# Transposing the attention output by DMA instead of on TensorE, and setting constants in pieces

## The chip, the cores and the metric

The kernel runs on one core of a Trainium2 chip. The metric is the device time of one execution in microseconds (us). The engines are called PE (TensorE, matrix engine), DVE (VectorE), ACT (ScalarE), POOL (GpSimd) and SP (the engine that only issues transfers here); PEld is the weight load of PE, which overlaps its matmuls (PE is busy for 98% of the span before, PEld for 65%).

The kernel before was timed with the changed one at 679.28 us (median of 4 runs, 679.05 to 679.72), and at 679.09 us when it stood alone.

## The reference, cut to what matters

```python
# attention: 4 batches, 8 heads, 768 positions, head width 64
# each query sees its window (|distance| < 16) and 24 block summaries (max of k, mean of v)
x = attn_out.transpose(0, 2, 1, 3).reshape(3072, 512)
P = np.exp(x @ w_gate - max)            # 8 experts
for _ in range(8):                       # the "normalisation"
    P /= P.sum(1, keepdims=True) + 1e-09
    P /= P.sum(0, keepdims=True) + 1e-09
    P *= N / E
for e in range(8):                       # experts, 512 -> 1024 -> 512
    out += P[:, e:e+1] * (np.maximum(x @ w1[e], 0) @ w2[e])
```

The gate products of this kernel (x @ w_gate) take the attention output with its 512 features on the partitions, that is, transposed. The attention produces it with positions on the partitions. Something has to transpose it: 16 head pairs (two heads of one batch), six blocks of 128x128 each.

## The kernel before

A planner in Python orders all work of the attention stage, with expert 0 as filler, before anything is emitted. It knows each unit by an engine, an estimated duration, its dependencies and a `lag`, the time that it believes passes between the end of a unit and the use of its result. The order in which an engine works is then fixed in the program: a unit that waits on the chip holds everything behind it on its engine (in the changed kernel PE is busy for 0.15 of the 2 us from 98 us on, while a gate product waits). Pairs 8 to 11 belong to batch 2, pairs 12 to 15 to batch 3.

```python
def to_xT(i, h=None):                      # six TensorE transposes into one PSUM bank
    t = at.pop(("xs", i, h or 0))
    tx = at["tx", i, h] = bank("a", "tx", FP16)
    for g in range(G if h is None else HG):
        nc.tensor.transpose(tx[:, g * 128:(g + 1) * 128],
                            t[:, g, :, :].rearrange("p j d -> p (j d)"), ident16)

def x_out(eng, i, h=None): ...             # copy PSUM -> xT on ACT or DVE

def near_values(i): ...                    # the four small "edge copies", SBUF to SBUF, issued from SP

def logits(b):                             # the gate products of batch b, 24 small matmuls
    lp = at["lp", b] = bank("a", "lp")[:, 0:G * E]
    ...

# in pair_whole(i), batches 1 to 3
U["xt", i] = add("PE", 0.35, lambda: to_xT(i), [U["no", i, 0], U["no", i, 1]], prio, opens=[buf])
U["x", i] = add({"ACT": 0.8, "DVE": 0.9}, 0, lambda: x_out(U["x", i].on, i), [U["xt", i]], prio, uses=[buf])
...
# after a batch: gate products, then the batch's filler
gate(b, xs, 900 if b < B - 1 else 0)
expert0(b * S, xs)
...
for i in range(4):                         # weights of expert 1, issued from POOL
    load(("w1n", i), lambda i=i: load_w1(1, i), 0.85, 1.3)
load("w2n", lambda: load_w2(1), 0.85, 5.0)
...
# in bridge(), the eight normalisation rounds: rows, by_rows (POOL), columns (DVE), totals (PE), ...
step = add(eng, us, fn, [step], -50.0, opens=o, uses=w, lag=(1.5 if n else 3.0) if fn is columns else 0.0)
```

The softmax here doesn't subtract the row's maximum and nothing guards it: scores larger than these inputs give would overflow.

Of the kernel before, what the change touches and what calls it, by code (L numbers as in the profile page):

```python
# [33 lines left out]
class Plan:  # L34
# [12 lines left out]
    def add(self, eng, cost, fn, deps=(), prio=0.0, opens=(), uses=(), lag=0.0):  # L47
        u = Unit(eng, cost, fn, [d for d in deps if d is not None], prio, list(opens), lag)
        for b in list(opens) + list(uses):
            b.users.append(u)  # L50
        if uses and eng != "PE":
            u.prio -= 100.0
        self.waiting.append(u)
        return u
# [62 lines left out]
def kernel(  # L117
# [10 lines left out]
    nc = tc.nc  # L128

    B, H, S, D = q.shape  # L130
    G = S // 128
    N, DM = out.shape
    E = moe_w_gate.shape[1]
# [5 lines left out]
    PB = H // 2  # L139
    SCALE = 1.0 / float(D) ** 0.5  # L140
    W = 16
# [4 lines left out]
    VD = D + 1  # L146
# [9 lines left out]
    col_en = const.tile([128, 128], FP32)  # L156
# [3 lines left out]
    xT = persist.tile([128, KD, N], FP16)  # L160
# [34 lines left out]
    def copy(eng, out, in_):  # L195
        (nc.scalar.copy if eng == "ACT" else nc.vector.tensor_copy)(out=out, in_=in_)
# [18 lines left out]
    NB = PB  # L215
    NE = 2
# [9 lines left out]
    if True:  # L226
# [4 lines left out]
        qT = [attn.tile([128, W + S + W], BF16, name=f"qT{i}") for i in range(NB)]  # L231
        kT = [attn.tile([128, S], BF16, name=f"kT{i}") for i in range(NB)]
# [6 lines left out]
        E_e = [attn.tile([128, G, 128], BF16, name=f"Ee{i}") for i in range(NE)]  # L239
        V_e = [attn.tile([128, G, 2 * VD], BF16, name=f"Ve{i}") for i in range(NE)]  # L240

        plan = Plan({"m": 3, "s": NS, "a": NA})
        add = plan.add

        at, units = {}, {}
# [49 lines left out]
        def tr(i, z, tag):  # L295
            st = at.pop(("st", i, z))
            t = at["t", i, z] = bank(tag, "tkq", BF16)
            for g in range(G):
# [4 lines left out]
                else:  # L303
                    nc.tensor.transpose(t[:, g * 128:(g + 1) * 128],  # L304
                                        st[:, g, :, :].rearrange("p j d -> p (j d)"), ident)

        def tr_out(eng, i, z):
            r, src = i % NB, at.pop(("t", i, z))[:, 0:S]
            dst = (kT[r][:], qT[r][:, W:W + S])[z]
            if i < PB:  # L310
                dst = dst.rearrange("c (p g) -> c p g", g=G)
                src = src.rearrange("c (g p) -> c p g", g=G)
            copy(eng, dst, src)
# [32 lines left out]
        def near_values(i):  # L346

            sv, ve = v_x[i % NQ], V_e[i % NE]
            for j in range(2):
                c0, q0 = VD * j, 64 + 32 * j  # L350
                nc.sync.dma_start(out=ve[q0 + W:q0 + 2 * W, 1:G, c0:c0 + VD],
                                  in_=sv[128 - W:128, j, 0:G - 1, :])
                nc.sync.dma_start(out=ve[q0:q0 + W, 0:G - 1, c0:c0 + VD],
                                  in_=sv[0:W, j, 1:G, :])

        def scores(i, h):
# [145 lines left out]
        def to_xT(i, h=None):  # L502
# [6 lines that stand above are left out]
        def x_out(eng, i, h=None):  # L509
            n, t0 = (S, 0) if h is None else (HS, h * HS)  # L510
            t0 += i // PB * S
            copy(eng, xT[:, i % PB, t0:t0 + n], at.pop(("tx", i, h))[:, 0:n])
# [76 lines left out]
            nc.vector.tensor_copy(out=wg_bf[:], in_=wg_f32[:])  # L589

        def late_constants():
            for t in E_e:
                nc.vector.memset(t[64:128, :, :], 0.0)
            for t in V_e:
                nc.vector.memset(t[:], 0.0)
                nc.vector.memset(t[0:24, :, D:VD], 32.0 / XS)
                nc.vector.memset(t[32:56, :, VD + D:2 * VD], 32.0 / XS)
            nc.vector.memset(col_en, float(E) / float(N))


        U = {}
# [20 lines left out]
        def pair_start(i, prio):  # L622
            o = i - NB
            war_k = [U.get(("S", o, 0)), U.get(("S", o, 1)), U.get(("km", o))]
            war_q = war_k[:2] + [U.get(("ss", o, 0)), U.get(("ss", o, 1))]
            tag = "m" if i < PB else "a"
            for z in range(2 if i >= PB else 1):
                buf = Buffer(tag)
                U["tr", i, z] = add("PE", 0.4, lambda z=z: tr(i, z, tag),
                                    [U["kq"[z], i], U["ident"]] + (war_k, war_q)[z]  # L630
                                    + [U["tr", i, 0] if z else U.get(("S", i - 1, 1 if i > PB else 0))],
                                    prio, opens=[buf])
                U["kT", i, z] = add({"ACT": 0.8} if z == 0 else {"ACT": 0.8, "DVE": 0.95},
                                    0, lambda z=z: tr_out(U["kT", i, z].on, i, z), [U["tr", i, z]], prio,
                                    uses=[buf])
            if i < PB:
                query_half(i, 0, prio)
            U["km", i] = add("DVE", 0.95, lambda: key_max(i), [U["kT", i, 0]] + war_q[2:], prio)
            buf = Buffer("a")
            U["vs", i] = add("PE", 0.4, lambda: block_sums(i),  # L640
                             [U["v", i]] + ([U.get(("A", i - NE, 1))] if i >= PB else []), prio + 0.01, opens=[buf])
            U["Vs", i] = add("DVE", 0.36 if i < PB else 0.84, lambda: block_out(i), [U["vs", i]],
                             prio + 0.01, uses=[buf])
# [37 lines left out]
            return U.get((what, n % PB, n // PB)) if n >= 0 else None  # L681

        def pair_whole(i, prio):
            U["near", i] = add("SP", 0.4, lambda: near_values(i), [U["v", i], U.get(("A", i - NE, 1))], prio,
                               lag=3.5)
            for h in range(2):
                buf = Buffer("s")
                U["S", i, h] = add("PE", 0.28, lambda h=h: scores(i, h),
                                   [U["kT", i, 0], U["kT", i, 1], U.get(("ed", i - 2))], prio, opens=[buf])
                U["X", i, h] = add("ACT", 0.97, lambda h=h: score_exp(i, h), [U["S", i, h]], prio, uses=[buf])  # L690
                U["mk", i, h] = add("DVE", 0.56, lambda h=h: masks(i, h),
                                    [U["X", i, h], U.get(("A", i - 2, 1))], prio)
            U["ed", i] = add("DVE", 0.78, lambda: edges(i),
                             [U["X", i, 0], U["X", i, 1], U["mk", i, 1], U.get(("A", i - NE, 1))], prio)
            bufs = [Buffer("a"), Buffer("a")]
            U["ss", i, 0] = U["ss", i, 1] = add("PE", 0.22, lambda: summaries2(i),
                                                [U["km", i], U["kT", i, 1], U.get(("A", i - NE, 1))], prio,
                                                opens=bufs)
            for h in range(2):
                U["sx", i, h] = add("ACT", 0.46, lambda h=h: summary_exp(i, h), [U["ss", i, h]], prio,  # L700
                                    uses=[bufs[h]])
            for h in range(2):
                buf = Buffer("a")
                U["A", i, h] = add("PE", 0.4, lambda h=h: values(i, h),
                                   [U["mk", i, h], U["ed", i], U["sx", i, h], U["Vs", i], U["near", i]],
                                   prio, opens=[buf])
                U["no", i, h] = add("DVE", 0.68, lambda h=h: normalize(i, h),
                                    [U["A", i, h], U.get(("xt", i - 2))], prio, uses=[buf])
            buf = Buffer("a")
            U["xt", i] = add("PE", 0.35, lambda: to_xT(i), [U["no", i, 0], U["no", i, 1]], prio, opens=[buf])  # L710
            U["x", i] = add({"ACT": 0.8, "DVE": 0.9}, 0, lambda: x_out(U["x", i].on, i), [U["xt", i]], prio,
                            uses=[buf])

        halves, zero = [], []

# [52 lines left out]
        c0 = add("DVE", 3.8, constants, [], -5.0)  # L768
        for i in range(PB):
            pair_start(i, i)  # L770
            pair_half(i, 0, i)
        add("DVE", 2.4, late_constants, [U["mk", PB - 1, 0]], 5.5)
        expert0(0, [U["x", i, 0] for i in range(PB)])
        for i in range(PB):
            pair_half(i, 1, 10 + i)
# [2 lines left out]
        for i in range(PB, NP):  # L778
# [3 lines left out]
            if i % PB == PB - 1:  # L782
                b = i // PB
                xs = [U["x", PB * b + d] for d in range(PB)]
# [24 lines left out]
    if True:  # L809
# [340 lines left out]
        g = q = NOTHING  # L1150
        for n in range(LAG, len(groups)):
            g0, q0 = g, q
            g = group(*groups[n])
            q = pair(*groups[n - LAG])
            e, j, i = groups[n]
# [55 lines left out]
        A, B, C, D = last  # L1211
# [42 lines left out]
```

## Time and profile before

| | before |
|---|---|
| time, median of 4 runs beside the changed kernel | 679.28 us |
| PE busy | 670.5 us, 98% of the span of the profiled run |
| transposes of attention outputs on PE | 96, six to a pair |
| DMA queue of SP, pairs 8 to 15 | edge copies only |

The prediction below shows the engine table, the stretches and the removed instructions.

One warning about this profile. The profiled execution took 684.06 us, some 5 us more than the others, because the clock fell near its start:

```profile
20.00:30.00 10.00, 9.02 (x108) 5.64 (x108) 6.78 (x22) 4.94 (x10) 5.27 (x7) 0.72 1.38 199
```

The columns are the stretch, its length, busy time and count of PE, PEld, DVE, ACT and POOL, the granted clock, the DMA share (the larger, the busier) and GB/s; here the clock was 0.72. A span is the time from the first to the last instruction on the core; it is some 2 us shorter than the device time.

### The profile page before, as it was taken

How to read it: one execution, taken by the hardware profiler on the slowest of the kernel's cores; microseconds unless marked ns; L12 is line 12 of the kernel's file. 1: busy time of each engine (PE TensorE's matmuls, PEld its weight loads, DVE VectorE, ACT ScalarE, POOL GpSimd, SP SyncE). 2: the span in 40 equal slices, each digit the busy share in tenths (PEclk: the TensorE clock that was granted, in tenths of full speed). 3: DMA queues.
4: the chain of work that ended last, by engine and by line, in shares of the span. 5: the costliest groups of instructions: out<-in, count | busy, mean ns of one | idle time of the engine just before them, and what ended most of it. 6: DMA issues, size and time to landing. Idle time of an engine off the chain costs nothing.

```text
span 681.4 us, 13654 instructions
## 1 busy us (share of the span) xinstructions
PE 670.5 (98%) x5189; PEld 441.6 (65%) x5189; DVE 585.4 (86%) x1445; ACT 407.7 (60%) x788; POOL 125.9 (18%) x165
## 2 busy tenths in 40 slices
PE   8999999999999999999999999999999999999996
PEld 4665666545666666666666666666666666666665
DVE  6778898788599988999889988998899888998886
ACT  4677877656677765555555555555555555555551
POOL 8699630022202010100101010201010101100000
PEclk9799999999999999999999999999999999999999
DMA  9999990000503123310513050404131051301224
GB/s 120 188 143 143 98 144 7 1 1 0 78 1 37 12 31 48 31 17 1 78 17 33 1 78 1 48 1 60 19 31 17 7 72 17 32 1 48 78 93 155
DMA packets 113618, 33.90 MB, mean 50 GB/s; under 512 B 99984, under 2 KB 110736, under 8 KB 113552
## 3 DMA queue, kind: packets, MB, share of 16 engines
q0 software_dynamic: 104672, 26.22, 41.6%
q1 hardware_dynamic: 8352, 6.80, 3.3%
q8 instruction: 40, 0.66, 0.4%
q14 instruction: 26, 0.21, 0.1%
q10 hardware_dynamic: 528, 0.02, 0.0%
HBM read 52.45 MB, written 6.29 MB: 86 GB/s over the span
## 4 chain that ended last, share of the span: by engine, by line
PE 92%; DVE 4%; DMA 1%; issue 1%; ACT 1%; POOL 1%; DVEq 0%; ACTq 0%
PE xy L883 36%; PE pg L877 16%; PE pa L877 10%; PE pb L877 10%; PE yps L210 6%; PE hps L200 6%; PE sg L323 1%; PE tkq L304 1%; PE vs L331 1%; PE av L468 1%; PE tx L506 1%; DMA qst<-in_q_dram 1%; DVE out_acc L1018 1%; PE av L395 1%; PE av L401 1%
## 5 line engine op out<-in xcount | busy, mean ns | idle before, releaser
L883 PEld LDWEIGHTS <-hf 128*128 128x128 f16 x2352 | 230.1, 98 | 96.1 <-issue 1.2
L883 PE MATMUL xy<-w,hf 128*128 128x256 f16 x1312 | 183.4, 273 | 0.1
L883 PE MATMUL xy<-ws,hf 128*128 128x256 f16 x984 | 147.6, 273 | 0.1
L191 ACT ACTIVATE hf<-pg 128x512 f16<-128x512 f32 x84 | 50.2, 597 | 149.6 <-PE pg L877 149.4
L1018 DVE SCALAR_TENSOR_TENSOR out_acc<-xy,P_sb,out_acc 128x512 f32<-128x512 f32 x164 | 115.1, 744 | 1.7 <-PE xy L883 1.7
L824 DVE TENSOR_TENSOR hf<-hf 128x512 f16<-128x512 f16 x252 | 99.6, 422 | 8.8
L877 PE MATMUL pa<-xT,w 128*128 128x512 f16 x336 | 99.9, 379 | 0.0
L877 PEld LDWEIGHTS <-w 128*128 128x128 f16 x672 | 65.8, 98 | 43.6 <-issue 0.6
L827 DVE TENSOR_TENSOR hf<-pb,c 128x512 f16<-128x512 f32 x84 | 58.1, 692 | 38.2 <-PE pb L877 35.7
L176 POOL DMA_DIRECT2D w<-in_moe_w_dram x56 | 41.8, 759 | 220.3 <-PE pg L877 192.1
L877 PEld LDWEIGHTS <-ws 128*128 128x128 f16 x504 | 49.3, 98 | 25.3
L911 ACT COPY c<-pg 128x512 f32<-128x512 f32 x84 | 49.2, 585 | 22.7 <-PE pg L877 22.6
L827 DVE TENSOR_TENSOR hf<-pg,c 128x512 f16<-128x512 f32 x84 | 57.2, 681 | 0.6 <-PE pg L877 0.6
L191 ACT ACTIVATE hf<-pa 128x512 f16<-128x512 f32 x84 | 50.6, 603 | 0.4 <-PE pa L877 0.4
L896 ACT COPY pg<-pa 128x512 f32<-128x512 f32 x84 | 47.9, 570 | 4.8
L877 PE MATMUL pg<-xTs,w 128*128 128x512 f16 x168 | 50.0, 379 | 0.1
L877 PE MATMUL pb<-xT,ws 128*128 128x512 f16 x168 | 50.0, 379 | 0.0
L877 PE MATMUL pg<-xTs,ws 128*128 128x512 f16 x168 | 50.0, 379 | 0.0
L877 PE MATMUL pg<-xT,w 128*128 128x512 f16 x168 | 50.0, 379 | 0.0
L877 PE MATMUL pb<-xTs,ws 128*128 128x512 f16 x168 | 50.0, 379 | 0.0
L904 ACT COPY c<-pb 128x512 f32<-128x512 f32 x84 | 49.8, 593 | 0.2 <-ACT pg L896 0.2
L200 PE MATMUL hps<-xT,w 128*128 128x384 f16 x256 | 48.7, 326 | 0.0
(136 smaller groups left out, 842.5 us busy)
## 6 DMA issues: line engine op xcount, KB each, us to landing
w<-in_moe_w_dram POOLq DMA_DIRECT2D x8, 1024.0 KB, 9.3
w<-in_moe_w_dram POOLq DMA_DIRECT2D x56, 128.0 KB, 3.5
out_dram<-out_acc SPq DMA_DIRECT2D x22, 256.0 KB, 2.0
qst<-in_q_dram POOLq DMA_DIRECT2D x32, 96.0 KB, 5.8
vx<-in_v_dram POOLq DMA_DIRECT2D x16, 192.0 KB, 6.5
kst<-in_k_dram POOLq DMA_DIRECT2D x24, 96.0 KB, 6.0
w<-in_moe_w_dram POOLq DMA_DIRECT2D x2, 512.0 KB, 8.3
kst<-in_k_dram POOLq DMA_DIRECT2D x4, 192.0 KB, 4.9
```

What stands on the lines that cost most here:

```text
L176: nc.gpsimd.dma_start(out=t[:, :, h, :], in_=moe_w1[e].rearrange("(dk p) f -> p dk f", p=128)[:, :, f:f + 128])
L191: nc.scalar.activation(out=out, in_=in_, func=AF.Relu, bias=0.0, scale=1.0)
L200: nc.tensor.matmul(hp[:, 0:n], lhsT=w1s[e][:, dk, 128 * f:128 * (f + 1)], rhs=xT[:, dk, t0:t0 + n], start=(dk == 0), stop=(dk == KD - 1))
L210: nc.tensor.matmul(yp[:], lhsT=h[:, f, c * 128:(c + 1) * 128], rhs=w2s[e][:, f, :], start=(f == 0), stop=(f == KF - 1))
L824: nc.vector.tensor_tensor(out=out, in0=in0, in1=in1, op=ALU.subtract)
L827: nc.vector.tensor_tensor(out=out, in0=in0, in1=in1, op=ALU.add)
L877: nc.tensor.matmul(bank[:], lhsT=w[:, dk, :], rhs=x[:, dk, :], start=start and dk == 0, stop=dk == KH - 1, skip_group_check=True)
L883: nc.tensor.matmul(bank, lhsT=a(f)[:, 128 * c:128 * (c + 1)], rhs=w[:, f, :], start=start and f == 0, stop=f == FH - 1, skip_group_check=True)
L896: nc.scalar.copy(out=B["g"][:], in_=B["a"][:])
L904: nc.scalar.copy(out=B["c5"][:], in_=B["b"][:])
L911: nc.scalar.copy(out=B["c2"][:], in_=B["g"][:])
L1018: nc.vector.scalar_tensor_tensor(out=acc, in0=src, scalar=P_sb[:, t, e:e + 1], in1=acc, op0=ALU.mult, op1=ALU.add)
```

## The change

The intent is to relieve PE, which bounds this stage: the outputs of pairs 8 to 15 are transposed by one DMA each, straight from SBUF to SBUF, so that 48 TensorE transposes, 8 evacuating copies and 8 uses of a PSUM bank go. The constants that later batches need are set as seven small units in place of one long one on DVE. Two further branches, for i >= 16, are never taken, since there are 16 pairs.

```diff
+        def x_dma(i):
+            nc.sync.dma_start_transpose(
+                out=xT[:, i % PB, i // PB * S:(i // PB + 1) * S].rearrange("c (g t) -> c g t", g=G),
+                in_=at.pop(("xs", i, 0))[:].rearrange("p g j d -> p (g j d)"))
...
         def late_constants():
-            for t in E_e:
-                nc.vector.memset(t[64:128, :, :], 0.0)
-            for t in V_e:
-                nc.vector.memset(t[:], 0.0)
+            def zero(t):
+                nc.vector.memset(t, 0.0)
+            def ones(t):
                 nc.vector.memset(t[0:24, :, D:VD], 32.0 / XS)
                 nc.vector.memset(t[32:56, :, VD + D:2 * VD], 32.0 / XS)
-            nc.vector.memset(col_en, float(E) / float(N))
+            parts = [(0.4, lambda t=t: zero(t[64:128, :, :])) for t in E_e]
+            for t in V_e:
+                parts += [(0.4, lambda t=t: zero(t[:])), (0.15, lambda t=t: ones(t))]
+            return parts + [(0.15, lambda: nc.vector.memset(col_en, float(E) / float(N)))]
...
-            buf = Buffer("a")
-            U["xt", i] = add("PE", 0.35, lambda: to_xT(i), [U["no", i, 0], U["no", i, 1]], prio, opens=[buf])
-            U["x", i] = add({"ACT": 0.8, "DVE": 0.9}, 0, lambda: x_out(U["x", i].on, i), [U["xt", i]], prio,
-                            uses=[buf])
+            if i >= 8:
+                U["xt", i] = U["x", i] = add("SP", 0.1, lambda: x_dma(i), [U["no", i, 0], U["no", i, 1]], prio,
+                                             lag=2.6)
+            else:
+                ...  # as before
...
-        add("DVE", 2.4, late_constants, [U["mk", PB - 1, 0]], 5.5)
+        c1 = U["mk", PB - 1, 0]
+        for us, fn in late_constants():
+            c1 = add("DVE", us, fn, [c1], 12.5)
```

More of the change, by code (lines that the diff above doesn't have):

```diff
@@ L305, in tr, with tr_dma @@
                                         st[:, g, :, :].rearrange("p j d -> p (j d)"), ident)
+        def tr_dma(i, z):
+            r, st = i % NB, at.pop(("st", i, z))
+            nc.sync.dma_start_transpose(out=(kT[r][:], qT[r][:, W:W + S])[z].rearrange("c (g t) -> c g t", g=G),
+                                        in_=st[:].rearrange("p g j d -> p (g j d)"))
+        def x_dma(i):
+            nc.sync.dma_start_transpose(
+                out=xT[:, i % PB, i // PB * S:(i // PB + 1) * S].rearrange("c (g t) -> c g t", g=G),
+                in_=at.pop(("xs", i, 0))[:].rearrange("p g j d -> p (g j d)"))
         def tr_out(eng, i, z):
@@ L350, in near_values @@
                 c0, q0 = VD * j, 64 + 32 * j
-                nc.sync.dma_start(out=ve[q0 + W:q0 + 2 * W, 1:G, c0:c0 + VD],
+                eng = nc.gpsimd if i >= 16 else nc.sync
+                eng.dma_start(out=ve[q0 + W:q0 + 2 * W, 1:G, c0:c0 + VD],
                                   in_=sv[128 - W:128, j, 0:G - 1, :])
-                nc.sync.dma_start(out=ve[q0:q0 + W, 0:G - 1, c0:c0 + VD],
+                eng.dma_start(out=ve[q0:q0 + W, 0:G - 1, c0:c0 + VD],
                                   in_=sv[0:W, j, 1:G, :])
@@ L627, in pair_start @@
             for z in range(2 if i >= PB else 1):
+                if i >= 16:
+                    U["tr", i, z] = U["kT", i, z] = add("SP", 0.1, lambda z=z: tr_dma(i, z),
+                                                        [U["kq"[z], i]] + (war_k, war_q)[z], prio, lag=2.6)
+                    continue
                 buf = Buffer(tag)
@@ L683, in pair_whole @@
         def pair_whole(i, prio):
-            U["near", i] = add("SP", 0.4, lambda: near_values(i), [U["v", i], U.get(("A", i - NE, 1))], prio,
+            U["near", i] = add(*(("POOL", 3.4) if i >= 16 else ("SP", 0.4)), lambda: near_values(i), [U["v", i], U.get(("A", i - NE, 1))], prio,
                                lag=3.5)
@@ L708, in pair_whole @@
                                     [U["A", i, h], U.get(("xt", i - 2))], prio, uses=[buf])
-            buf = Buffer("a")
-            U["xt", i] = add("PE", 0.35, lambda: to_xT(i), [U["no", i, 0], U["no", i, 1]], prio, opens=[buf])
-            U["x", i] = add({"ACT": 0.8, "DVE": 0.9}, 0, lambda: x_out(U["x", i].on, i), [U["xt", i]], prio,
-                            uses=[buf])
+            if i >= 8:
+                U["xt", i] = U["x", i] = add("SP", 0.1, lambda: x_dma(i), [U["no", i, 0], U["no", i, 1]], prio,
+                                             lag=2.6)
+            else:
+                buf = Buffer("a")
+                U["xt", i] = add("PE", 0.35, lambda: to_xT(i), [U["no", i, 0], U["no", i, 1]], prio, opens=[buf])
+                U["x", i] = add({"ACT": 0.8, "DVE": 0.9}, 0, lambda: x_out(U["x", i].on, i), [U["xt", i]], prio,
+                                uses=[buf])
         halves, zero = [], []
```

## The prediction

> **What bounds the kernel now.** I read the engine table first, then the chain that ended last, then the engines stretch by stretch, and last the order of time around the instructions that the change removes. The engine table and the head of the chain:
>
> ```profile
> PE 670.5 (98%) x5189; PEld 441.6 (65%) x5189; DVE 585.4 (86%) x1445; ACT 407.7 (60%) x788; POOL 125.9 (18%) x165
> ...
> PE 92%; DVE 4%; DMA 1%; issue 1%; ACT 1%; POOL 1%; DVEq 0%; ACTq 0%
> ```
>
> The matrix engine is busy for 98% of the span, and 92% of the chain that set the end is its work. An average can hide stages, so I read the busy time of each engine in stretches (columns: stretch, its length, busy time and count of PE, PEld, DVE, ACT, POOL, then the clock, the DMA column and GB/s):
>
> ```profile
> 45.00:66.00 21.00, 21.00 (x235) 13.12 (x234) 18.66 (x52) 15.81 (x25) 20.45 (x25) 1.00 2.47 143
> 66.00:88.00 22.00, 21.92 (x262) 13.79 (x260) 19.85 (x53) 18.03 (x30) 15.21 (x19) 1.00 1.63 106
> 88.00:109.00 21.00, 21.00 (x253) 13.44 (x252) 17.80 (x48) 16.26 (x27) 3.44 (x5) 1.00 0.82 102
> 109.00:130.00 21.00, 21.00 (x226) 12.83 (x224) 15.79 (x43) 14.22 (x23) 0.00 (x0) 1.00 0.02 4
> 130.00:178.00 48.00, 46.82 (x260) 24.56 (x257) 36.33 (x94) 27.78 (x56) 11.42 (x18) 1.00 0.00 1
> ```
>
> Attention of batches 2 and 3 lies at about 80 to 130 us, with expert 0 woven between as filler. The matrix engine has no idle time in the two stretches from 88 to 130, although the vector engine is at 75 to 85%. So in this stage a microsecond taken off the matrix engine is a microsecond off the time, and one taken off ACT or DVE alone is worth nothing. From 130 to 178 us the eight rounds of the routing normalisation run on DVE and POOL, filled by the rest of expert 0; there 1.2 us are idle. After 178 us the order is untouched by the change. The DMA engines are nearly silent after 109 us, which matters for the new transfers.
>
> The removed work is told by the view of the tile that holds the transposed attention output, and by one spot in order of time (start, length, engine, line):
>
> ```profile
> L506 PE MATMUL tx<-ident,xs x96: 216/219/314, 13.2 to 127.9; 128*128 128x128 f16 x96
> L196 ACT COPY xT<-tx x15: 460/798/805, 13.7 to 128.2; 128x768 f16<-128x768 f16 x10, 128x384 f16<-128x384 f16 x5
> ...
> 105.94 1.04 PE L210 MATMUL yps<-w,h 128*128 128x512 f16 x4
> 106.81 0.50 PE L506 MATMUL tx<-ident,xs 128*128 128x128 f16 x6
> 107.14 1.03 PE L210 MATMUL yps<-w,h 128*128 128x512 f16 x4
> ```
>
> The 219 ns of one transpose is latency, not the engine's cost: six of them started at 106.81 and the next matmul started at 107.14, so six take the engine 0.33 us (about 55 ns each). The neighbours are dense: four 512-wide matmuls take 106.81 - 105.94 = 0.87 us, 217 ns each.
>
> [...] for plain transfers from SP: 2.0 us median for 256 KB, and 1.9 us for the fastest of the small edge copies; but those edge copies take 4.6 us in the median, issued while the load queue is full:
>
> ```profile
> out_dram<-out_acc SPq DMA_DIRECT2D x22, 256.0 KB, 2.0
> Ve<-vx SPq DMA_DIRECT2D x48, 10.2 KB, 4.6
> ```
>
> No trace of this case shows a crossbar transpose yet.
>
> **The change part by part.** There are 4 batches of 8 heads, so 16 head pairs, numbered 0 to 15. The two branches under "i >= 16" (keys and queries by DMA, edge values issued from POOL) are therefore never taken; the built program confirms it: POOL has the same instruction count and the transposes of keys and queries stay on the matrix engine. Two parts remain.
>
> Part one, outputs of pairs 8 to 15. Removed: 8 x 6 = 48 matrix-engine transposes (96 fall to 48 in the built program), 8 evacuating copies of 128x768 (0.8 us on ACT or 0.56 us on DVE), and 8 uses of a PSUM bank. Added: 8 transposing transfers of 128x768 two-byte values (192 KB) on SP. On the path: 8 x 0.33 = 2.65 us; some groups are followed a little later (0.43 us to the next start at 122.74), so I take 2.8 us. The 8 copies, at most 6.4 us of ACT, are off the path. The scheduler moves part of the query copies from DVE to ACT and output copies the other way, which again is not on the path.
>
> What replaces them is a delay. Only the gate products of batches 2 and 3 wait first for the new transfers; the expert products of the batch stand behind them in the order. Batch 3 is the tight one. In the built order 16 output matmuls (16 x 0.217 = 3.5 us) and 4 hidden matmuls (4 x 0.163 = 0.65 us) stand between the last value product and the gate product: 4.1 us. In the trace of before, the last value product is out of the way at 125.89, and the last normalised output is written at 126.67 + 0.56 = 127.23, 1.34 us later. So a transfer may take 4.1 - 1.3 = 2.8 us from issue to landing before the matrix engine stalls. For batch 2 the same count (two score groups, one block-sum, two transposes, 16 hidden matmuls: some 4.3 us) leaves about 3.0 us. [...] the change itself plans 2.7 us. That fits in the slack, just. I charge 0.4 us for the two places together.
>
> Part two, constants in pieces. In the trace of before the block of memsets holds DVE in one go while the matrix engine runs dummy work and then has real gaps:
>
> ```profile
> 23.62 1.91 PE L544 MATMUL idle<-zeros 128*128 128x512 bf16 x4
> 23.90 0.38 DVE L593 MEMSET Ee<- 64x384 uint32 x1
> ...
> 25.89 0.17 DVE L598 MEMSET col_en<- 128x128 f32 x1
> ...
> 27.18 0.39 PE L323 MATMUL sg<-qT,kT 64*128 64x160 bf16 x8 [0.40 <-ACT qT L196]
> ...
> 29.04 0.33 PE L506 MATMUL tx<-ident,xs 128*128 128x128 f16 x3 [0.58 <-ACT es L430]
> ```
>
> I cannot see the memsets delay a matmul directly: they end at 26.06, before the next normalisation starts at 26.36. The four dummy matmuls stay in the new order. What changes is that the scheduler now believes DVE free and puts the transposes of pair 3 ahead of the summary scores, and 4 hidden matmuls into the place where the engine waited 0.58 us for ACT. Of the 1.0 us of waits at 27.2 and 29.0 I expect 0.6 us back.
>
> A third effect: the new order puts the first normalisation product 4 hidden matmuls (0.65 us) nearer to the end of attention, while its DVE and POOL chain is as long as before. At 139.9 the trace already has a 0.9 us wait of this kind. I charge 0.3 us.
>
> Sum: -2.8 - 0.6 + 0.4 + 0.3 = -2.7 us. From 679.1 that is 676.4 us.
>
> **The rivals.** (1) The gain turns into a stall. [...] the gate products of both batches each wait about 5 us: +10 - 3.4, some 686 us. For it: nothing of the kind has been measured here[...]. Against it: one instruction carries all six blocks[...], and the change plans 2.7 us. At 4.5 us, a middle case, each place loses 1.6 us and the time is about 679 us, no change. (2) The bound moves: with the matrix engine relieved, DVE at 75 to 90% or the normalisation chain becomes the bound, and nothing or 1 us is won: 678 to 679 us. Against it: the copies on DVE hardly change in number in the new order (two more of outputs, two fewer of queries), and it has a fifth of its time free between 88 and 130. (3) The SP queue[...] holds edge copies behind a transpose that still waits for its data; the value products then wait. The order speaks against it: the edge copies that follow a transpose belong to a pair two to three ahead. It would cost below 2 us, 678 us. (4) The reordering helps more than counted, as pieces of filler land in other small gaps: 674 us.
>
> **Range and chances.** The removable work is 2.8 us and the visible gaps of the stage about 1 us, so 674.3 is the low end. The high end, 679.3, allows a transfer of some 4.5 us, or stalls that eat the gain. A gain of 2% would be 13.6 us, four times what is removed; a loss of 2% needs a transfer near 10 us at both places. Predicted 676.4 us, range 674.3 to 679.3; faster 0.01, same 0.97, slower 0.02.
>
> **What would show it.** Right: 48 instead of 96 of the tx transposes; the gate products of batches 2 and 3 with waits under 0.5 us; a landing time of 2.5 to 3 us for the new transfers; attention ending (the first row sums of the routing) 3 us before the 130.49 us of the old trace; the same length from there to the end. Wrong: a gate product waiting over 1 us on the transfer; landings of over 4 us; the row sums 3 us earlier but the output matmuls of expert 1 (start at 176.3 us) not, which would mean that the normalisation chain took the gain; or the matrix engine idle in the stretches from 88 to 130 us.

The sum stands: -2.8 - 0.6 + 0.4 + 0.3 = -2.7 us, that is 676.4 us from 679.1. The +0.4 us and the wait of 5 us in rival 1 are suppositions.

## More of the kernel before

One more view is needed later: what PE waited for (line of the waiting instruction, what it waited for: us in total, times, longest).

```profile
PE sink L1077 <- DVE csum_sb L1072: 0.9, 1, 0.9
...
PE tx L506 <- ACT es L430: 0.6, 1, 0.6
...
PE sg L323 <- ACT qT L196: 0.4, 1, 0.4
```

"sink" is the total over all rows in one normalisation round, "csum_sb" the column sums that feed it. There are few waits, and none of them is for a transfer in the attention of batches 2 and 3.

## The result, and the profile after

The changed kernel took 687.84 us (median of 4 runs, 687.32 to 688.62), against 679.28 us of the kernel before in the same session. The ratio is 1.0126, with a 95% interval of 1.0109 to 1.0144. Ratios here are the mean time of one kernel's fast runs over that of the other's from the same rounds, so they are not quite the ratio of the medians. The change made the kernel 8.6 us slower. That is within the band of 2% that the prediction thought almost certain, but outside its range, and it has the other sign.

PE did lose the work (page of the changed kernel, busy time by engine):

```profile
PE 668.6 (98%) x5141; PEld 437.2 (64%) x5141; DVE 581.7 (85%) x1440; ACT 404.2 (59%) x785; POOL 125.9 (18%) x165
```

5141 matmuls are the 5189 of before less 48, and DVE and ACT lose five and three instructions, together the eight copies. But one stretch stands out, first the changed kernel, then its stand-in for before, the run with the pieces alone (span 677.3 us, mean clock 0.998, nothing in its attention outputs changed; stretches, columns as above):

```profile
88.00:109.00 21.00, 15.61 (x160) 9.88 (x160) 11.66 (x32) 9.93 (x17) 0.94 (x2) 0.84 0.91 111
```

```profile
88.00:109.00 21.00, 21.00 (x256) 13.27 (x254) 18.62 (x50) 16.32 (x26) 0.00 (x0) 1.00 0.51 70
```

In the same 21 us PE is idle for 5.4 us, the clock averages 0.84, and 160 matmuls are done in place of 256. The waits of PE in the changed kernel say for what:

```profile
PE lp L531 <- DMA xT<-xs: 5.4, 2, 3.6
PE sink L1102 <- DVE csum_sb L1097: 1.8, 2, 1.0
...
PE ss L430 <- DVE xT L196: 0.5, 1, 0.5
...
PE sg L333 <- ACT qT L196: 0.4, 1, 0.4
```

"lp" are the gate products, "xT<-xs" the new transfers. The order of time shows where (start, length, instruction, what it waited for in brackets):

```profile
96.03 0.20 PE L531 MATMUL lp<-wg_bf,xT 128*128 128x8 f16 x2
99.85 0.18 PE L531 MATMUL lp<-wg_bf,xT 128*128 128x8 f16 x1 [3.62 <-DMA xT<-xs]
101.80 0.72 PE L531 MATMUL lp<-wg_bf,xT 128*128 128x8 f16 x21 [1.76 <-DMA xT<-xs]
...
103.40 2.74 PE L200 MATMUL hps<-xT,w 128*128 128x384 f16 x8
```

All of it is at the gate of batch 2. The eight hidden matmuls at 103.40 then take 2.74 us, where the same group took 1.46 us at 94.73. The stretches around it say why (same columns):

```profile
98.00:100.00 2.00, 0.15 (x1) 0.10 (x1) 0.00 (x0) 0.00 (x0) 0.00 (x0) 1.00 1.45 129
100.00:102.00 2.00, 0.23 (x8) 0.21 (x8) 0.00 (x0) 0.00 (x0) 0.00 (x0) 0.87 0.65 112
102.00:104.00 2.00, 2.00 (x32) 1.09 (x30) 0.00 (x0) 1.13 (x3) 0.00 (x0) 0.50 0.00 0
104.00:106.00 2.00, 2.00 (x8) 0.97 (x7) 0.00 (x0) 1.15 (x3) 0.00 (x0) 0.50 0.00 0
106.00:108.00 2.00, 2.00 (x25) 1.79 (x23) 1.65 (x5) 0.25 (x1) 0.00 (x0) 0.50 0.00 0
```

After the wait the granted clock is 0.50 for 6 us, with PE busy throughout. This stall of 5.4 us costs 5.4 us and then some 3 us more.

Last, the transfers. Issues from SP in order of time, and then the issues and landings of the stretch from 80 to 96 us (KB each, median us from issue to landing):

```profile
88.45 1.34 SPq L313 DMA_TRANSPOSE xT<-xs  x1
...
93.58 0.59 SPq L364 DMA_DIRECT2D Ve<-vx  x1
94.27 1.76 SPq L313 DMA_TRANSPOSE xT<-xs  x1
```

```profile
w<-in_moe_w_dram POOLq DMA_DIRECT2D x8, 128.0 KB, 6.8
w<-in_moe_w_dram POOLq DMA_DIRECT2D x1, 1024.0 KB, 13.0
...
xT<-xs SPq DMA_TRANSPOSE x3, 7.5
```

The four transfers of batch 2 landed 6.9, 7.4, 11.3 and 7.5 us after their issue, and the four of batch 3 after 3.4, 2.8, 4.5 and 2.8 us. Those of batch 2 fly beside other loads: the first mostly beside those of the attention, the others beside the weights of expert 1 too, which are issued from 81.22 us on (2 MB as landed). The large load was issued at 88.04 and, with 13.0 us, landed at 101.0; the last two transposes landed at 99.8 (88.5 + 11.3) and 101.8 (94.3 + 7.5), which are the two moments when PE could go on.

From the first gate product (40.13 us) to the first output product of expert 1 (179.57 us) the changed kernel takes 139.44 us; the stand-in takes 132.47 us. The difference of 6.97 us adds up from what the views show: 5.4 of waiting, 3.1 of half clock (6 us at 0.50 and 2 us at 0.93), less 2.65 of removed transposes (as the prediction measured them), plus 1.0 more of waiting in the normalisation (1.8 in place of a 0.8 us wait on DVE in the stand-in): 6.85 us.

From there to the end the changed kernel takes 506.13 us against 504.64. The order of time has six gaps of some 0.24 us each in front of weight loads of the output products, 1.4 us together, whose releaser the profile doesn't show ("issue"); the stand-in has none of these six.

### The profile page after: what moved, and what is told of

Its sections match the earlier page's. It is cut to its first block, busy times and chain, and to the rows that moved or that the text cites. A ratio compares the mean times of both kernels' runs of the same rounds, so it can differ in the third digit from the quotient of the medians.

```text
span 685.7 us, 13574 instructions
## 1 busy us (share of the span) xinstructions
PE 668.6 (98%) x5141; PEld 437.2 (64%) x5141; DVE 581.7 (85%) x1440; ACT 404.2 (59%) x785; POOL 125.9 (18%) x165
## 4 chain that ended last, share of the span: by engine, by line
PE 90%; DVE 6%; DMA 2%; issue 1%; POOL 0%; ACT 0%; DVEq 0%; ACTq 0%; POOLq 0%
PE xy L908 36%; PE pg L902 16%; PE pb L902 10%; PE pa L902 10%; PE yps L210 6%; PE hps L200 5%; DMA xT<-xs 1%; PE tkq L304 1%; PE sg L333 1%; DVE out_acc L1043 1%; DMA vx<-in_v_dram 1%; PE vs L341 1%; PE av L406 1%; DVE xs L510 1%; PE ss L430 1%
## 5 line engine op out<-in xcount | busy, mean ns | idle before, releaser
L200 PE MATMUL hps<-xT,w 128*128 128x384 f16 x256 | 50.1, 333 | 0.0
```

The costliest lines, as they stand in the source:

```text
L200: nc.tensor.matmul(hp[:, 0:n], lhsT=w1s[e][:, dk, 128 * f:128 * (f + 1)], rhs=xT[:, dk, t0:t0 + n], start=(dk == 0), stop=(dk == KD - 1))
```

## The experiments

The theories that the expectations name: **A**, the gate of batch 2 waits for transposes that share the DMA engines with loads, and after the wait the clock is at half (0.50 for 6 us in the changed kernel); **B**, a transposing transfer ("the crossbar" in the expectations) is slow by itself; **C**, the order of issue on SP makes it late; **D**, the constants in pieces and the new order are the loss. All twelve runs gave correct results. Medians are of 4 runs, or of 6 where five rounds were run (the planned wait again, and the three runs on the normalisation). The kernel before, run beside them, had a median of 680.18 us in the session of the pieces alone, batch 3 alone, the load moved and the dummies; 679.93 us in that of the transposes alone, the issue order, both together and the planned wait; 679.85 us with the normalisation, and 679.99 us in the last. Single runs of several kernels, the kernel before too, have a mean clock of 0.988 to 0.995; most of them are 1 to 7 us longer than the other runs of their kernel, which widens the intervals.

### Each part alone

The pieces alone:

```diff
-            if i >= 8:
+            if i >= 99:
```

> Only the constants in pieces; all outputs are transposed on the matrix engine as before. Theory A (the loss is the wait for the transfers of batch 2, whose DMA engines are full of loads, plus the half clock after it): this part is harmless, 678.3 to 679.8 us. Theory D (the pieces and the new order they bring do the harm): 683 us or more.

Measured: 679.4 us, ratio 0.9991 (0.9976 to 1.0006). D falls: with the pieces alone nothing is lost.

The transposes alone, the constants in one block as before:

```diff
-        c1 = U["mk", PB - 1, 0]
-        for us, fn in late_constants():
-            c1 = add("DVE", us, fn, [c1], 12.5)
+        add("DVE", 2.4, late_constants, [U["mk", PB - 1, 0]], 5.5)     # and the old late_constants
```

> The other part alone: transposes of batches 2 and 3 by DMA, the late constants set in one block as before. Theory A: all of the loss is here, 686.5 to 689 us. Theory D (constants in pieces and the order that follows are the loss): about 680 us.

Measured: 684.84 us, ratio 1.006 (1.003 to 1.0089). Most of the loss is here, by the medians 4.9 of the 8.6 us, but not all, and my 686.5 to 689 was too high: the interval lies below that of the changed kernel, so some 3 us come only with both parts together, though the pieces alone lose nothing. The planner laid the order differently: the gate waits 4.5 us in place of 5.4, the small gaps after 180 us sum to 0.35 us in place of 1.41, the totals of the normalisation wait 2.2 us in place of 1.8, and the clock is again 0.50 for 6 us. By stretches, the 2.5 us between the spans of the two profiled runs (685.7 and 683.2) are 1.3 us before the first gate product (38.83 us in place of 40.13; 467 matmuls come before it in place of 483, so part of this is work moved behind it), 0.1 us from there to expert 1, and 1.1 us after.

### Transposes where nothing else is in flight

Only batch 3 by DMA:

```diff
-            if i >= 8:
+            if i >= 12:
```

> Transfers for batch 3 only (4 of 8), pieces kept. Theory A: these run while the loads are over; they land in 2.8 to 4.5 us as in the changed kernel, the gate product waits under 0.5 us, 1.4 us of matrix work is saved: 677 to 679 us, no half clock. Theory B (the crossbar is slow by itself, whatever else runs): half of the loss stays, about 683 us.

Measured: 679.57 us, ratio 0.9994 (0.9979 to 1.0009), no wait at a gate. The view of the issuing line shows the landings of its four transfers:

```profile
DMA to landing us min/median/max: 2.8/2.8/3.1
```

This is nearly the 2.7 us that the change plans and that the prediction counted on. B falls: the same instruction with the same amount of data is not slow by itself (2.8 to 3.1 us here, 6.9 to 11.3 us for batch 2 in the changed kernel). The time that I expected, 677 to 679 us, did not come: from the first gate product to expert 1 the run takes 132.40 us, the stand-in 132.47. The totals of the normalisation wait 1.8 us here, where the stand-in has one wait of 0.8 us, so most of the 1.3 us of removed transposes is lost again.

### The load moved away from batch 2

POOL issues the expert-1 weights only after it has read from the last output of batch 2:

```diff
+        def hold_weights():
+            nc.gpsimd.tensor_copy(out=hold_t[:], in_=xT[0:1, (12 - 1) % PB, 2 * S:2 * S + 8])
+        last[0] = add("POOL", 0.2, hold_weights, [last[0], U["x", 11]])
         for i in range(4):
             load(("w1n", i), lambda i=i: load_w1(1, i), 0.85, 1.3)
```

> All 8 transfers, but POOL reads the last transposed output of batch 2 before it issues the 9 weight loads of expert 1 (3 MB read), so that these no longer share the DMA engines with the transfers of batch 2. Theory A: landing of the last two transfers of batch 2 falls from 7.5 and 11.3 us to 3 to 5 us, the gate product waits under 1 us, the clock stays full: 676 to 679 us. Theory B (slow crossbar) or C (the issue order on SP): the wait stays over 4 us, 686 us or more.

Measured: 681.33 us, ratio 1.0021 (1.0003 to 1.004): most of the loss is gone. But the time is above the 676 to 679 us that I expected, and the wait above 1 us. (The expectation also has the size of the load wrong: by the reference's sizes 4 MB are read, not 3.) The slow landings moved with the load. Batch 2's transfers landed in 2.8 to 6.2 us, the slowest being the first, which flies beside the loads of the attention, and the slowest of all eight, 7.3 us, is now one of batch 3, beside the weights that are issued from 99 us on. What is left of the wait at the gate is short, and the clock stays at 1.00 (waits of PE, then a stretch):

```profile
PE lp L532 <- DMA xT<-xs: 1.5, 1, 1.5
```

```profile
88.00:109.00 21.00, 19.53 (x235) 12.29 (x234) 16.79 (x47) 15.18 (x25) 7.00 (x10) 1.00 0.78 81
```

### The half clock taken away, the stall left

Twenty dummy matmuls in front of the gate products of batch 2 keep PE busy in the first part of the stall, some 4.3 us by an estimate from the 217 ns that a 512-wide matmul takes in the trace of before (in the profile of this run PE is busy without a gap from 94 to 100 us, and 1.4 us of the wait are left):

```diff
+            if b == 2:
+                for _ in range(20):
+                    nc.tensor.matmul(t[:], lhsT=zeros[:], rhs=zeros[:, None, :].to_broadcast([128, 4, 128]),
+                                     start=True, stop=True)
```

> The changed kernel with 20 dummy 512-wide matmuls[...] put ahead of the gate products of batch 2, inside the wait of 5.4 us. They remove no wait. If the half clock after the wait is a cost of its own (matmuls of 128x384 took about 0.32 us each for 6 us after it, 0.16 before), it goes and the time falls by about 3 us to 684 to 685.5 us. If the wait alone costs, the time stays at 687 to 688.5 us.

Measured: 686.38 us, ratio 1.0102 (1.0064 to 1.0139); of its four runs two at a clock of 0.999 to 1.000 took 684.61 and 684.96 us, as expected; the others fell in clock, and the median misses the 684 to 685.5 us. In the profiled one the gate products came no earlier than in the changed kernel (the last of them from 102.01 us on, there from 101.80), but the clock stayed up:

```profile
102.00:104.00 2.00, 1.99 (x36) 1.38 (x37) 0.00 (x0) 1.13 (x3) 0.00 (x0) 1.00 0.00 0
```

The way from the first gate product to the first output product of expert 1 is 137.02 us, 2.4 us shorter than in the changed kernel. The half clock is thus a cost of its own, of about 2.4 to 3 us, and the stall is the rest.

### The issue order on SP

In the changed kernel the last transfer of batch 2 was issued at 94.27 behind four edge copies, though its data was there at 92.90. Here the edge copies depend on the transfer two pairs earlier, so it goes first:

```diff
-[U["v", i], U.get(("A", i - NE, 1))]
+[U["v", i], U.get(("A", i - NE, 1)), U.get(("xt", i - 2)) if i >= 10 else None]
```

> The changed kernel, but from pair 10 on the edge copies of a pair depend on the transposing transfer two pairs earlier, so that on SP the transfer is issued ahead of them. The order on the matrix engine is that of the changed kernel. Theory A: the last transfer of batch 2 starts about 1.4 us earlier, the wait at the gate product shrinks from 5.4 to about 4 us, the half clock stays, and the time is 685 to 687.5 us. Theory C (issue order on SP is what makes it late): the wait goes and the time is about 680 us.

Measured: 686.8 us, ratio 1.0091 (1.0058 to 1.0124). C falls. The size that I gave for A was wrong too: I had expected the wait to shrink by 1.4 us, and it didn't:

```profile
102.50 0.72 PE L531 MATMUL lp<-wg_bf,xT 128*128 128x8 f16 x21 [5.28 <-DMA xT<-xs]
```

The transfer was issued at 93.79, half a microsecond earlier, and landed 8.7 us later, at 102.5, with the load still around it. It left at once this time (its data was there at 93.77, 0.9 us later than in the changed kernel, which is why only 0.5 us were won). Issued earlier, it did not land earlier.

Both together, weights held back and edge copies behind:

> Both together: the expert-1 weights are loaded only after the transfers of batch 2, and the edge copies are issued behind the transposing transfers. Theory A: the wait of 1.5 us that was left with the weights held back (where the last transfer had stood behind four edge copies on SP) goes, and the time falls by 1 to 1.5 us below that run, to 679.5 to 680.5 us, level with the kernel before, not below it by more than 1 us. If the transfers do have a gain of 2.8 us to give, as the prediction had it, 677 to 678 us.

Measured: 681.24 us, ratio 1.001 (0.9979 to 1.0041). The wait at the gate fell from 1.5 to 0.9 us, less than the expected 1.5, and the time missed the 679.5 to 680.5 us. It is level with the kernel before within the interval, and no gain.

### The wait planned, the contention left

The planner is told a transfer time for batch 2 that is nearer to what the trace showed:

```diff
-                                             lag=2.6)
+                                             lag=2.6 if i >= 12 else 8.0)
```

> The changed kernel, but the planner is told 8.0 us instead of 2.6 us for the transfers of batch 2 (pairs 8 to 11), so it puts the gate products of batch 2 later and other work in front of them. Nothing is said to the chip about the traffic: the weight loads, the edge copies and the transfers stay as they are. Theory A (the loss is the matrix engine waiting for transfers that share the DMA engines with loads, and then running at half clock): the transfers still land in 6 to 11 us, but no gate product waits over 1 us, the clock stays full, and the time is 678.5 to 681 us. Rival (the transfers cost the matrix engine something beyond the wait, or the new order is worse): still 684 us or more.

Measured: 679.6 us, ratio 0.9996 (0.9963 to 1.0029). The transfers of batch 2 are as slow as ever (view of the issuing line, up to 99 us):

```profile
DMA to landing us min/median/max: 6.2/7.4/11.4
```

Yet no gate product waits, since the planner put other work in front: the gate of batch 2 starts at 104.31 us, and the stretch is full and at full clock:

```profile
88.00:109.00 21.00, 21.00 (x246) 12.91 (x243) 17.70 (x48) 16.40 (x28) 0.76 (x1) 1.00 1.03 123
```

One number in the planner undoes the whole loss of 8.6 us. It is the strongest evidence for A: the slow transfers harm only where PE stands and waits for them. But the 2.7 us that were to be won don't appear either. The waits of PE in this run:

```profile
PE sink L1102 <- DVE csum_sb L1097: 2.2, 2, 1.4
```

The same program in five rounds:

> The same program as the planned-wait run, timed in five rounds, since its first interval (0.9963 to 1.0029) hardly tells a gain of 2.7 us (ratio 0.9960) from none. If the gain that the prediction counted on is there once the stall is planned away: 0.995 to 0.997. If the normalisation rounds (2.2 us of waits at their totals in that run's profile, none with the pieces alone) and the small stalls later take it: 0.9985 to 1.001.

Measured: 679.14 us against 679.99, ratio 0.9994 (0.9978 to 1.0009), as the second reading has it: a gain of 2.7 us (0.9960) is excluded. Measured from the first gate product to the first output product of expert 1, the planned kernel takes 131.49 us in its first profile and 131.92 in this one, 1.0 and 0.55 us less than the stand-in. Of the 2.65 us of removed transposes 1.4 us go to the totals of the normalisation (2.2 us of waits in place of the stand-in's one wait of 0.8), which leaves 1.25. Another 0.7 us is lost after that (505.32 us to the end in the first profile against 504.64; small gaps of unknown cause sum to 0.42 of it). The profile of the kernel before has 505.08 us in this last stretch, so most of the 0.7 is not a loss against it.

### Can the normalisation give the gain back?

The planner is told that the column sums of the first two rounds come later, so that more matrix work stands in front of the totals:

```diff
-lag=(1.5 if n else 3.0) if fn is columns else 0.0
+lag=(4.5, 3.0, 1.5)[min(n, 2)] if fn is columns else 0.0
```

On top of the planned wait:

> The run with the planned wait (8.0 us for the transfers of batch 2), and on top of it the planner is told that the column sums of the first two normalisation rounds come later (4.5 and 3.0 us in place of 3.0 and 1.5), so that it puts more matrix work in front of the first two totals. In the planned-wait run these two totals held the matrix engine for 0.78 and 1.41 us. If that wait is what ate the 2.65 us of removed transposes: the waits at the totals fall below 0.3 us each and the time is 677 to 678.2 us, ratio about 0.997 against the kernel before. If the freed time is lost elsewhere (small stalls later, or the filler running out near 178 us): 679 to 680 us, no difference.

As a control, on the kernel before:

> A control: the kernel before, with nothing but the two later column sums of the normalisation. Its first total waits 0.9 us in the trace. If the later totals help by themselves: about 0.9 us faster, 678 to 679 us; if that wait only moves: 679.3 to 680.3 us. What the transposes by DMA add is the difference between this run and the planned run with the later column sums.

With batch 3 alone by DMA:

> Only batch 3 transposed by DMA (no load in flight there), with the two later column sums. If half of the removed transposes (1.3 us) come through once the chain no longer takes them: 677.7 to 679 us, between the control and the planned run; if not: as the control.

Measured: 682.15 us, ratio 1.0025 (1.0003 to 1.0047); 682.38 us, ratio 1.0043 (1.001 to 1.0077); 681.69 us, ratio 1.003 (0.9998 to 1.0062). The first two expectations missed. The third came true in its second reading: the run is as the control, and the half of the gain didn't come through. Low clocks are part of these medians, but not all: the runs with a mean clock of 0.998 or more took 680.3 and 681.5 us, 680.72 to 681.52, and 680.0 and 680.4, those of the kernel before 678.74 to 680.52. The waits at the totals did go, in each of the three, but another came (waits of PE in the first of them):

```profile
PE pg L902 <- DVE xT L849: 2.3, 1, 2.3
```

"pg" is a product of expert 1, and xT a difference of attention outputs that DVE forms for it, in place. In the control the same wait is 2.3 us, in the batch-3 run 2.6 us. So in this short stretch a wait of PE for DVE that was removed in one place came back in another. In the batch-3 run the clock then fell too, though the wait is far shorter than the stall of the changed kernel (a stretch just after it, columns as above):

```profile
139.00:140.00 1.00, 1.00 (x4) 0.42 (x3) 0.69 (x2) 0.00 (x0) 0.00 (x0) 0.50 0.00 0
```

No version that I ran beats the kernel before beyond its interval; the best, the planned wait, the pieces alone and batch 3 alone, equal it.

## Why the prediction was wrong, point by point

**PE bounds the stage, and 2.8 us of it go.** The removed work is right: 48 transposes and 8 copies. That PE bounds the stage was right up to the gate of batch 3, but only as long as nothing else is late. What counts for a full engine is the spacing: 55 ns for a transpose here, with 219 ns of latency. The six blocks of a pair take 0.33 us of PE against 2.8 us by DMA at best, 8.5 times as long.

**The delay of the transfers.** This is the step that failed: "For batch 2 the same count ... leaves about 3.0 us", set against "the change itself plans 2.7 us", with the conclusion "That fits in the slack, just. I charge 0.4 us for the two places together." For batch 3 it held: landings of 2.8 to 4.5 us and no wait at its gate. For batch 2 the term of 0.4 us measured 5.4 us, as the transfers took 6.9 to 11.3 us. The slack itself was about right (the last output was there at 92.90, and PE ran out of other work at 96.2), but the last transfer spent 1.4 us of it behind edge copies before its issue. The 2.7 us hold for DMA engines with little else to move (2.8 to 3.1 us with batch 3 alone), and I had supported the charge with "The DMA engines are nearly silent after 109 us", while batch 2's transfers run from 76 to 102 us. The stretches that I showed have 106 and 102 GB/s there, and I had even written that the edge copies take 4.6 us "issued while the load queue is full". The page of before also has 6.5 us as the median landing of the loads of vx, 192 KB each as the new transfers. The evidence was on the page; it was read for the wrong batch. That the figure fits the quiet case so well is partly luck: no trace had shown a transposing transfer, and only the 2.0 and 1.9 us of plain transfers from SP stood behind it.

**The cost of a stall.** I counted a microsecond of stall as a microsecond. The two waits, 3.6 and 1.8 us with one matmul between them, were followed by 6 us at a clock of 0.50, 2.4 us by the run with dummies and 3.1 us by the clock column. Waits of 5.3 us (the edge copies behind) and of 3.6 and 1.8 us were followed by a clock of 0.50, one of 1.5 us (the load moved) was not. But waits of 2.9 and 1.6 us (the transposes alone) and a single one of 2.6 us (batch 3 with the later column sums) were followed by it too, two others of 2.3 us were not, and in the profile of before the clock fell at 15.2 us after waits of 0.7, 0.3 and 0.5 us. So the length of a single wait doesn't decide it; what does is not shown here. Nor did the work that followed bring the full clock back at once: in the changed kernel PE was busy from 101.8 us on and the clock stayed at 0.50 until 108.3 us, some 6.5 us. Summed from stretches of 0.1 us, the half clock lasted 6.83 us in the changed kernel and 10.24 us in the profile of before; by stretches of 2 us it lasted some 6.8 us with the transposes alone and with the edge copies behind.

**What would show it.** The prediction had named a gate product waiting over 1 us and landings of over 4 us as signs of being wrong, and both came. The row sums, which should have begun 3 us earlier than 130.49, began at 133.36 us. (The 130.49 us are from the profile in which the clock fell; in the stand-in they begin at 126.95, so they are 6.4 us late.)

**Rival 1** was the right one in kind, "The gain turns into a stall", and its 686 us was near. Its reason was not: it took the transposing transfer to be slow by itself, at both batches, with a wait of 5 us that was a supposition, and I put it aside with "the change plans 2.7 us". A plan is no measurement. Of **rival 3**, edge copies held up on SP, nothing shows: in the changed kernel no value product waits for one.

**The range.** Two of its sums are off: 2.8 us of removable work and 1 us of gaps give 675.3 us as the low end, not 674.3; and with slacks of 2.8 and 3.0 us a loss of 2% needs transfers of some 11 us at both places, not 10. Neither would have saved the prediction.

**Constants in pieces, -0.6 us.** The time of the pieces alone, -0.6 us with an interval of about 1 us to each side, neither shows nor excludes it. The waits speak for less: the 0.58 us wait for ACT went and left one of 0.16 us, the 0.40 us wait stayed, and one of 0.50 us came at 69.4 us.

**The third effect, +0.3 us,** points the right way and is too small; that the four moved matmuls are its reason was not tested. The totals of the normalisation wait 1.8 us in the changed kernel against 0.9 before, and 2.2 us once the stall is planned away. I had rival 2, the normalisation chain as the new bound, at "678 to 679 us" and unlikely; with the stall planned away it is what takes about half of the gain.

**What stays open** are the gaps of about 0.24 us in front of weight loads after 180 us: six in the changed kernel (1.4 us), none with the pieces alone, two to six in others. The control of the normalisation, which has no transposing transfer at all, has seven, and takes 506.23 us from expert 1 to the end, so the transfers are not needed for them. They recur at the same places of the program in several kernels, but the profile names no releaser, and no run here tells their cause.

The account of the 8.4 us between the spans of the changed kernel (685.7) and the stand-in (677.3) is then: 5.4 stall, about 3 half clock, -2.65 transposes, 1.0 normalisation, 1.4 small gaps, together some 8.2 us. The stall and the half clock are shown by the runs; the removed work is reckoned from the trace of before.

## What to carry to other kernels

Before work is moved from an engine to a DMA, read the landing times of transfers in the very stretch where the new ones will fly, not a figure from a plan, and give the planner that figure: 192 KB landed in 2.8 to 3.1 us in the quiet (batch 3 alone), and in 6.9 to 11.3 us beside the loads of the attention and 2 MB of weights. In a fixed order a consumer that comes too early turns slow transfers into a stall of the bounding engine, and here a stall of 4.5 to 5.4 us cost some 3 us more through the clock of TensorE, which was then at 0.50 for some 6.8 us; once the clock fell after a wait of 2.6 us (batch 3 with the later column sums). A microsecond taken off the bounding engine is worth a microsecond only as far as the next chain has slack: here, once the stall was planned away, 1.4 of the 2.65 us of removed transposes went into waits at the totals of the normalisation.
